# Running sums of two of seven block products kept in PSUM by ScalarE copies instead of VectorE adds, in a fused attention and MLP kernel

## The chip, the cores and the metric

The kernel runs on one core of a Trainium2 chip. The metric is the device time of one execution in microseconds; the lower the better. Before the change the median of 3 runs was 529.97 us (529.93 to 530.95).

## What is computed

Attention over 2 batches of 12 heads, 448 positions and 64 dimensions a head, then two MLPs on the 896 x 768 result, all in float32:

```python
x = attention(q, k, v)            # 896 x 768
h = ((x @ w1) * (x @ w2)) @ w3    # 896 x 1024
x = h @ w_out                     # 896 x 768
g = np.maximum(x @ w_in, 0.0) ** 2   # 896 x 2048
out = g @ w_out2                  # 896 x 768
```

## The kernel before

Each large product after the attention is done as a 2 x 2 block product with seven block products in place of eight (P1 to P7, a Strassen-Winograd form), issued in the order 1, 2, 6, 5, 7, 3, 4. Every float32 operand of a block product is split into a high part (a cast to the matmul's reduced float32, by ScalarE) and a low part (float32 minus high part, by VectorE), and each block product is three matmuls: high by high, high by low, low by high.

The change is in the last product, `g @ w_out2`. The 2048 columns of `g` are worked off in four groups, `g` = 0 to 3 in the code. A group has two stretches. In the first, the products with `win2` make four 448-row tiles of `g` for both halves of the batch, each squared and split. In the second (called the o stretch below), `o_step` multiplies them with `w_out2`. For each block product n there are two halves d of the inner dimension, and for each d three row tiles t = 0, 1, 2 of 128 rows. Every (n, d, t) is three matmuls of 128 x 128 by 128 x 384, so a block product is 18 matmuls in a group. The last 64 rows of each batch half are done by `rest_step` in two tiles, 24 matmuls in a group; together 150.

PSUM has eight banks. A row tile t uses three accumulation chains (`CHAIN`): "a" holds P1, then P1+P2; "b" starts as a ScalarE copy of P1 and then takes P6, P7 and P4; "c" holds P5, then P5+P3. When a block product of a tile is done, the bank is added to the running sum of the output tile in SBUF (`into_acc`, `acc_tile`; these tiles are named `g0` in the built program and `g` in the profile). The first time a tile is met it is copied, by whichever of ScalarE and VectorE the planner chooses; each later time it is a VectorE `tensor_tensor` add (line 1182, recorded at the helper's line 425). P2 goes to tile (t, 0), P6 and then P5+P3 to tile (3+t, 0), P5 and then P1+P6+P7 to tile (3+t, 1), and P4's bank to tile (t, 1). Because the chain in bank b goes on after it has been read out, P7's matmuls of a tile wait for the read of P6, and P4's for the read of P7; in chain c P3's wait for the read of P5.

The rest tiles are done otherwise already: in groups 1 to 3 ScalarE copies the running sum into the bank first (line 1248), the matmuls add to it, and ScalarE copies it out.

The order on each engine comes from `Program.order`, a list planner with fixed costs per operation that runs once when the program is built. Engines work through their lists in that order. ScalarE (ACT), VectorE (DVE) and the sync engine's DMA queue (SP) each take the next instruction only when the one ahead has started. `prog.add` records an operation with its engines, what it reads and what it writes; `act`, `dve` and `pe` give the planner's costs. `take_bank` and `take_fs` hand out a PSUM bank or one of twelve SBUF rows (`fs`).

Of the kernel before, what the change touches and what calls it, by code (L numbers as in the profile page):

```python
# [8 lines left out]
F32 = mybir.dt.float32  # L9
# [115 lines left out]
def attention_moe_moe2(ctx: ExitStack, tc: tile.TileContext, qk, v, w1, w2, w3, w_out, w_in2, w_out2, out):  # L125
    nc = tc.nc
    NP_ALL, P, S2 = qk.shape
# [11 lines left out]
    HN = DM // 2  # L139
# [24 lines left out]
    fs = big.tile([P, NFS, S], F32, tag="fs", name="fs")  # L164
# [6 lines left out]
    def mm(o, l, r, start, stop, **more):  # L171
        return nc.tensor.matmul(o, l, r, start=start, stop=stop, **more)  # L172
# [41 lines left out]
    GROUPS = KF2 // 4  # L214
    TT = S // P
# [118 lines left out]
    prog = Program({"S": 700})  # L334
    pools = {}
    engine_of = {"A": nc.scalar, "V": nc.vector}

    def act(width, psum=False, strided=False):
        gap = 60 + 0.815 * width if psum else 75 + (0.96 if strided else 0.845) * width
        return {"A": (gap, gap + 105)}  # L340

    def dve(width, fast=False):
        gap = 70 + (0.52 if fast else 1.038) * width
        return {"V": (gap, gap + 85)}
# [3 lines left out]
    def pe(columns):  # L348
        return {"T": (columns * PE_ROW, columns * PE_ROW + 170)}
# [3 lines left out]
    def bank(i):  # L353
        if i not in banks:
            pool, tag = (pools["ps"], "mm") if i < 6 else (ps_w, "w")
            banks[i] = pool.tile([P, S], F32, tag=tag, name=f"bank{i}")
        return banks[i]

    free_banks = list(range(8))
    written = [0] * 8  # L360
# [5 lines left out]
    tiles = {}  # L366
# [21 lines left out]
    def g_at(kind, at, parts, width):  # L388
        m, at = divmod(at, ROW)
        if m < EVEN:  # L390
            m, at = 0, m * ROW + at
        if (kind, m) not in tiles:
            tiles[kind, m] = pools["big2"].tile(
                [P, ROW if m else EVEN * ROW], F32 if (kind, m) == ("g", 0) else F32R, tag=f"G{m}", name=f"{kind}{m}")
        return tiles[kind, m][:, at:at + parts * width].rearrange("p (s c) -> p s c", s=parts)

    def g_names(at, width):
        return [("g", c) for c in range(at // REST, (at + width) // REST)]

    def acc_tile(i):  # L400
        return g_at("g", i * HN, 1, HN)[:, 0]
# [22 lines left out]
    def tt(out, x, y, what):  # L424
        return lambda e: engine_of[e].tensor_tensor(out(), x(), y(), op=what)  # L425
# [5 lines left out]
    def copy(out, x):  # L431
        return lambda e: engine_of[e].copy(out(), x()) if e == "A" else engine_of[e].tensor_copy(out(), x())  # L432
# [12 lines left out]
    def fs_at(i, width=S):  # L445
        return lambda: fs[:, i, :width]

    def bank_at(i, width=S):
        return lambda: bank(i)[:, :width]
# [331 lines left out]
    def end_attention(e):  # L781
        attention.close()
        for n in ("xt", "big2"):
            pools[n] = ctx.enter_context(tc.tile_pool(name=n, bufs=1, reuse_waits="tile"))
        pools["ps"] = ctx.enter_context(tc.tile_pool(name="ps", bufs=6, space=PSUM, reuse_waits="tile"))
        for i in range(6):
            bank(i)
        for n in B_OF.values():
            tiles["x", n] = xB.get(n) or pools["xt"].tile([P, 2, KH, S], F32R, tag=n, name=f"x{n}")

    prog.add({"T": (0, 0)}, end_attention, [], [("open",)], behind=prog.ops)
    for c in range(2):
        place = turn("w", 2)
# [24 lines left out]
    def slot_in(n, k):  # L818
        return {"T1": 0, "T3": KH, "T2": 2 * KH, "B21": 3 * KH}[n] + k

    for n in ("B21", "T2", "T1", "T3"):
        for k in range(KH):
            i = slot_in(n, k)
# [3 lines left out]
    for k in range(KH):  # L827
        i, b = slot_in("T2", k), slot_in("B21", k)
# [88 lines left out]
    def ring_names(u):  # L917
        k = slot_of[u]
        return [("ring", i, s) for i in ((k, k + 1) if wide(u) else (k,)) for s in "hl"]
# [3 lines left out]
    def take_bank():  # L923
        return free_banks.pop(0)

    def take_fs():
        return free_fs.pop(0)
# [83 lines left out]
    def need_block(g, n, d):  # L1011

        if (g, n, d) in g_place:
            return
        at = g_place[g, n, d] = place_at(turn("place", PLACES))
        m = 4 * g + 2 * d
        b11, b12, b21, b22 = (g_rows[m + i, 1 - b] for i in range(2) for b in range(2))

        def sub(out, x, y):
            prog.add(dve(BN), tt(fs_at(out, BN), fs_at(x, BN), fs_at(y, BN), ALU.subtract),  # L1020
                     [("fs", x), ("fs", y)], [("fs", out)])

        row = {"1": b11, "2": b21, "5": b11, "7": b12, "3": b22, "4": b21}.get(n)
        if n == "6":
            row = take_fs()
            sub(b11, b12, b11)
            sub(row, b22, b11)
        elif n == "7":
            sub(b12, b22, b12)
        his, los = (g_names(at + r * BN, BN) for r in range(2))  # L1030
        parts_of(lambda: g_at("g", at, 2, BN)[:, 0], lambda: g_at("g", at, 2, BN)[:, 1], fs_at(row, BN), BN, ("fs", row),
                 his, los)
        if n == "6":
            sub(b21, b21, row)
        if n not in "12":
            give_fs(row)
# [140 lines left out]
    def into_acc(g, tile, n, bk, final):  # L1177

        i = 2 * tile + n
        o, a, src, dst = bank_at(bk, HN), lambda: acc_tile(i), ("bank", bk), g_names(i * HN, HN)  # L1180
        if (tile, n) in begun:
            prog.add(dve(HN), tt(a, o, a, ALU.add), [src, *dst], dst)
        else:
            begun.add((tile, n))
            prog.add(act(HN, True) | (dve(HN) if tile < 2 * TT else {}), copy(a, o), [src], dst)
        if final and g == GROUPS - 1:
            cols = slice(n * HN, (n + 1) * HN)
            if tile < 2 * TT:
                chunks = [(slice(0, P), (1 - tile // TT) * S + tile % TT * P)]
            else:  # L1190
                chunks = [(slice(b * REST, (b + 1) * REST), b * S + BN) for b in range(2)]
            for ps, row in chunks:
                prog.add({"S": (200, 2000)}, lambda e, ps=ps, row=row: nc.sync.dma_start(
                    out=out[row:row + ps.stop - ps.start, cols], in_=acc_tile(i)[ps]), dst)

    begun, o_state, rest_bank = set(), {}, {}

    def o_step(n, g, d, t, unit):

        need_block(g, n, d)  # L1200
        st = o_state.setdefault((g, t), {})
        w, at, chain = hls[unit], g_place[g, n, d], CHAIN[n]
        start = chain not in st
        if start:
            st[chain] = take_bank()
            written[st[chain]] = HN
            if n == "1":
                assert written[free_banks[0]]
                st["b"] = take_bank()
                written[st["b"]] = HN  # L1210
        i = st[chain]

        def run(e):
            x = g_at("g", at, 2, BN)
            for s, r in ((0, 0), (0, 1), (1, 0)):
                mm(bank(i)[:, :HN], x[:, s, t * P:(t + 1) * P], w[r],
                   start and (s, r) == (0, 0), d == 1 and (s, r) == (1, 0), skip_group_check=True)

        prog.add(pe(3 * HN), run, ring_names(unit) + g_names(at, 2 * BN) + ([] if start else [("bank", i)]),
                 [("bank", i)])  # L1220
        if d == 0:
            return
        if n == "1":
            j = st["b"]
            prog.add(act(HN, True), copy(bank_at(j, HN), bank_at(i, HN)), [("bank", i)], [("bank", j)])
        elif n == "2":
            into_acc(g, t, 0, i, True)
        elif n in "63":
            into_acc(g, TT + t, 0, i, n == "3")
        elif n in "57":  # L1230
            into_acc(g, TT + t, 1, i, n == "7")
        else:
            into_acc(g, t, 1, i, True)
        if n in "234":
            free_banks.append(i)
# [28 lines left out]
    for at, (kind, what, which, used) in enumerate(plan):  # L1264
        for u in used:
            need_unit(u)
        if kind == "product":
            product(what, which, used[0], at == 0)
        elif kind == "h":
            h_step(what, *which, used[0])  # L1270
        elif kind == "o":
            o_step(what, *which, used[0])
        else:
            rest_step(*what, which, used[0])
# [53 lines left out]
```

## Time and profile before

| what | value |
|---|---|
| median of 3 runs | 529.97 us (529.93 to 530.95) |
| the profiled execution's own time | 529.73 us |
| its span (first to last instruction) | 528.0 us |
| between the two | 1.73 us |
| TensorE (PE) busy | 514.4 us, 97% of the span |
| VectorE (DVE) busy | 490.8 us, 93% |
| ScalarE (ACT) busy | 385.4 us, 73% |
| granted TensorE clock | 1.00 |

PEld is TensorE's weight load, which runs beside the matmul before it. An instruction's duration in the trace is longer than its pitch (the distance from its start to the next one's start on a busy engine), because ends and starts overlap. "Idle before" is time in which the engine had nothing running, with what ended the wait behind an arrow.

### The profile page before, as it was taken

Reading aid. Unit: us, or ns where it says so; the run is one execution under the profiler, and the core shown is the slowest. Engines: PE = TensorE matmul, PEld = TensorE weight load, DVE = VectorE, ACT = ScalarE, POOL = GpSimd, SP = SyncE. Lnnn points to the kernel's source line nnn. Section 1 sums busy time; section 2 is a strip of 40 time slices with the busy share of each in tenths; the row PEclk is TensorE's granted clock in tenths of the full one; section 3 lists DMA queues with packets and bytes.
Section 4 is the critical chain, followed back from the end, with each engine's and each line's share of the span. In section 5 each row is a group of like instructions: output and inputs, shape, how many; then the busy total and the mean of one; then the engine's idle time right before and its main releaser. Section 6 shows DMA issues by size and latency. Waiting matters only on the chain.

```text
span 528.0 us, 8458 instructions
## 1 busy us (share of the span) xinstructions
PE 514.4 (97%) x2905; PEld 461.2 (87%) x2905; DVE 490.8 (93%) x1157; ACT 385.4 (73%) x890; POOL 15.2 (3%) x20
## 2 busy tenths in 40 slices
PE   6899999999999999999999999999999999999995
PEld 4658888888879999999999999999999989988995
DVE  5999998989899999987975899999999999999996
ACT  5989988767779465638486478986896589649951
POOL 1000000000000010221100000000000000000000
PEclk9999999999999999999999999999999999999999
DMA  8956544352652569999752402405530544044114
GB/s 315 303 194 227 178 170 175 124 178 69 236 176 65 179 186 253 251 251 258 164 164 89 153 27 65 175 1 177 182 122 0 164 172 145 0 127 175 59 60 150
DMA packets 26571, 81.29 MB, mean 154 GB/s; under 512 B 2400, under 2 KB 13408, under 8 KB 26528
## 3 DMA queue, kind: packets, MB, share of 16 engines
q1 hardware_dynamic: 22752, 75.24, 42.4%
q0 software_dynamic: 3776, 5.51, 6.6%
q8 instruction: 23, 0.38, 0.3%
q14 instruction: 20, 0.16, 0.1%
HBM read 74.84 MB, written 14.55 MB: 169 GB/s over the span
## 4 chain that ended last, share of the span: by engine, by line
PE 72%; DVE 19%; ACT 5%; DMA 2%; issue 1%; DVEq 0%
PE bank L172 51%; PE w L172 11%; DVE g L425 6%; PE s L172 4%; PE x L172 3%; PE pp L695 3%; DVE ring L425 3%; DVE fs L425 2%; DVE xs L486 2%; ACT ring L432 2%; DVE p L653 2%; DVE xs L425 1%; DMA raw_w<-in_w 1%; ACT xs L478 1%; DVE p L680 1%
## 5 line engine op out<-in xcount | busy, mean ns | idle before, releaser
L432 ACT CAST ring<-xs 128x384 fp32r<-128x384 f32 (+1 forms) x194 | 102.7, 546 | 48.8 <-PE bank L172 19.4
L172 PE MATMUL bank<-xT,ring 128*128 128x448 f32 x630 | 132.0, 366 | 0.0
L172 PEld LDWEIGHTS bank<-xT,ring 128*128 128x128 f32 x630 | 117.7, 188 | 9.4
L425 DVE TENSOR_TENSOR ring<-xs,ring 128x384 fp32r<-128x384 f32 (+1 forms) x194 | 111.4, 588 | 12.1 <-ACT ring L432 11.8
L172 PE MATMUL bank<-ring,g 128*128 128x384 f32 x600 | 106.1, 336 | 1.3 <-DVE g L425 1.3
L172 PEld LDWEIGHTS bank<-ring,g 128*128 128x128 f32 x600 | 104.1, 188 | 3.0 <-DVE g L425 2.6
L172 PE MATMUL bank<-xB,ring 128*128 128x448 f32 x489 | 102.9, 366 | 0.1
L172 PEld LDWEIGHTS bank<-xB,ring 128*128 128x128 f32 x489 | 91.4, 188 | 8.5 <-DVE ring L425 0.9
L663 ACT ACTIVATE p<-p,st 112x224 f32<-112x224 f32 (+3 forms) x96 | 50.1, 536 | 10.1 <-DVE st L653 10.1
L425 DVE TENSOR_TENSOR xs<-xs 128x384 f32<-128x384 f32 x96 | 51.7, 551 | 0.1
L432 ACT CAST g<-fs 128x384 fp32r<-128x384 f32 (+1 forms) x88 | 35.4, 421 | 14.9 <-DVE fs L425 14.7
L653 DVE CUSTOM_DVE_ANT_0 p<-s,mask 112x224 f32<-112x224 f32 (+3 forms) x96 | 36.8, 444 | 6.3 <-PE s L172 6.2
L172 PE MATMUL w<-hl_wout,w 128*128 128x384 f32 x192 | 36.2, 340 | 0.6 <-DVE wraw L425 0.6
L425 DVE TENSOR_TENSOR g<-fs,g 128x384 fp32r<-128x384 f32 (+1 forms) x88 | 36.7, 430 | 0.0
L172 PEld LDWEIGHTS w<-hl_wout,w 128*128 128x128 f32 x192 | 32.8, 188 | 1.9 <-DVE fs L425 0.9
L478 ACT ACTIVATE xs<-raw_w 128x768 f32<-128x768 f32 (+1 forms) x30 | 24.3, 816 | 11.6 <-DMA raw_w<-in_w 5.8
L172 PE MATMUL s<-qk 64*112 64x448 f32 (+3 forms) x192 | 28.0, 436 | 4.7 <-DMA qk<-in_qk 4.7
L432 ACT COPY fs<-bank 128x448 f32<-128x448 f32 x49 | 26.1, 532 | 8.1 <-PE bank L172 8.1
L425 DVE TENSOR_TENSOR g<-bank,g 128x384 f32<-128x384 f32 x60 | 31.5, 551 | 0.0
L172 PE MATMUL bank<-ab,ring 128*128 128x448 f32 x144 | 29.5, 365 | 0.0
L680 DVE TENSOR_SCALAR p<-p,st 112x448 f32<-112x448 f32 (+1 forms) x96 | 29.1, 360 | 0.1
L172 PEld LDWEIGHTS bank<-ab,ring 128*128 128x128 f32 x144 | 27.0, 188 | 2.1
(77 smaller groups left out, 667.6 us busy)
## 6 DMA issues: line engine op xcount, KB each, us to landing
raw_wout<-in_w_out SPq DMA_DIRECT2D x24, 768.0 KB, 4.3
raw_w<-in_w SPq DMA_DIRECT2D x16, 768.0 KB, 4.9
raw_win<-in_w_in SPq DMA_DIRECT2D x16, 768.0 KB, 4.3
raw_w<-in_w SPq DMA_DIRECT2D x16, 512.0 KB, 4.4
qk<-in_qk SPq DMA_DIRECT2D x12, 448.0 KB, 5.1
s_dram<-w_dram POOLq DMA_DIRECT2D x8, 576.0 KB, 9.1
w_dram<-wraw SPq DMA_DIRECT2D x8, 384.0 KB, 2.4
s_dram<-w_dram SPq DMA_DIRECT2D x4, 768.0 KB, 7.3
```

The source lines that it names most:

```text
L172: return nc.tensor.matmul(o, l, r, start=start, stop=stop, **more)
L425: return lambda e: engine_of[e].tensor_tensor(out(), x(), y(), op=what)
L432: return lambda e: engine_of[e].copy(out(), x()) if e == "A" else engine_of[e].tensor_copy(out(), x())
L478: nc.scalar.activation(y(), raws[key][:, :, 1].bitcast(F32), AF.Prelu, scale=2.0 ** -112, alpha=-2.0 ** 32)
L486: nc.vector.scalar_tensor_tensor(yi, yi, 3, raws.pop(key)[:, :, 0], op0=ALU.logical_shift_left, op1=ALU.bitwise_or)
L653: prog.add({"V": (gap, gap + 160)}, lambda e: nc.vector.tensor_tensor_reduce(block(p, j, i), s_t[p, j, g][:CP, o:o + w], mask[:, S - w:], ...
L663: prog.add({"A": (gap, gap + 100)}, lambda e, i=i: nc.scalar.activation(block(p, j, i), block(p, j, i), AF.Exp, bias=st_t[p][:, 0, j, i:i ...
L680: lambda e, i=i: nc.vector.tensor_scalar(block(p, j, i), block(p, j, i), st_t[p][:, 3, j, i:i + 1], None, ALU.mult),
L695: nc.tensor.transpose(x[0][:CP, o * CP:(o + 1) * CP], block(p, j, i)[:, c * CP:(c + 1) * CP], ident[:CP, :CP])
```

## The change

P5 and P3 are taken out of the VectorE adds, except in the last group.

- P5: a running sum of its own, in a new SBUF tile `P5` for t = 0 and 1 and in an `fs` row for t = 2. In groups 1 to 3 ScalarE copies the sum into the bank (`sum_in`) before P5's first matmul, which then adds to it. In groups 0 to 2 ScalarE copies it out again (`sum_out`) and the bank is given back. In group 3 the bank holds P5 of all groups and goes to tile (3+t, 1) by `into_acc` as before, and P3 is added on top of it in the same bank.
- P3: in groups 0 to 2 it has a chain of its own, "e". ScalarE copies tile (3+t, 0) into a bank, P3's matmuls add to it, and ScalarE copies it back.
- Tile (3+t, 1) is now met first by P7, so in group 0 P7 is a copy where it was an add.

```diff
@@ end_attention
+        tiles["P5"] = pools["xt"].tile([P, TT - 1, HN], F32, tag="P5", name="P5")
@@
+    def sum_in(i, x, names):
+
+        prog.add(act(HN), copy(bank_at(i, HN), x), names, [("bank", i)])
+
+    def sum_out(i, x, names):
+        prog.add(act(HN, True), copy(x, bank_at(i, HN)), [("bank", i)], names)
+
+    def p5_sum(t):
+
+        if t < TT - 1:
+            return lambda: tiles["P5"][:, t], ("P5", t)
+        if "row" not in p5_row:
+            p5_row["row"] = take_fs()
+        return fs_at(p5_row["row"], HN), ("fs", p5_row["row"])
...
+        over = g == GROUPS - 1
+        if n == "3" and not over:
+            chain = "e"
         start = chain not in st
         if start:
             st[chain] = take_bank()
+            assert written[st[chain]]
             written[st[chain]] = HN
...
-        i = st[chain]
+        i, to = st[chain], 2 * (TT + t)
+        if start and n == "5" and g:
+            sum_in(i, p5_sum(t)[0], [p5_sum(t)[1]])
+            start = False
+        elif start and n == "3":
+            sum_in(i, lambda: acc_tile(to), g_names(to * HN, HN))
+            start = False
...
         elif n == "2":
             into_acc(g, t, 0, i, True)
+        elif n == "3" and not over:
+            sum_out(i, lambda: acc_tile(to), g_names(to * HN, HN))
+        elif n == "5" and not over:
+            sum_out(i, p5_sum(t)[0], [p5_sum(t)[1]])
+            free_banks.append(i)
         elif n in "63":
             into_acc(g, TT + t, 0, i, n == "3")
```

TensorE's list is the same before and after but for the bank numbers. On VectorE, in the o stretch of group 2, these are the rows from the first add of P5 to the first add of P7 before the change (`g0<-bank` is an add to a running sum, `g3` to `g7` are low parts of the left operand, `ring` low parts of the weights):

```order
L425 TENSOR_TENSOR g0_3549<-bank7_2196,g0_3549 128x384
L425 TENSOR_TENSOR g7_3581<-fs_70,g7_3581 128x384
L425 TENSOR_TENSOR ring_68<-xs_69,ring_68 128x384
L425 TENSOR_TENSOR xs_69<-xs_69 128x384
L425 TENSOR_TENSOR g0_3549<-bank1_1959,g0_3549 128x384
L425 TENSOR_TENSOR g0_3549<-bank3_1961,g0_3549 128x384
L425 TENSOR_TENSOR ring_68<-xs_69,ring_68 128x384
L425 TENSOR_TENSOR g7_3581<-fs_70,g7_3581 128x384
L425 TENSOR_TENSOR fs_70<-fs_70 128x384
L425 TENSOR_TENSOR ring_68<-xs_69,ring_68 128x384 x2
L425 TENSOR_TENSOR g0_3549<-bank5_1963,g0_3549 128x384
```

and these the rows of the same place after it:

```order
L425 TENSOR_TENSOR xs_69<-xs_69 128x384
L425 TENSOR_TENSOR g7_3582<-fs_70,g7_3582 128x384
L425 TENSOR_TENSOR xs_69<-xs_69 128x384
L425 TENSOR_TENSOR g7_3582<-fs_70,g7_3582 128x384
L425 TENSOR_TENSOR ring_68<-xs_69,ring_68 128x384
L425 TENSOR_TENSOR fs_70<-fs_70 128x384
L425 TENSOR_TENSOR ring_68<-xs_69,ring_68 128x384 x3
L425 TENSOR_TENSOR g0_3550<-bank5_1964,g0_3550 128x384
```

P5's three adds are gone, and P7's first add (the last row of either) stands that much earlier in the list.

On ScalarE, in the same o stretch, from a cast of the left operand to the last cast before the raw weights of the next group, before the change:

```order
L432 CAST g5_3371<-fs_70 128x384
L432 CAST g7_3581<-fs_70 128x384 x2
L432 COPY g0_3549<-bank2_1960 128x384
L432 CAST ring_68<-xs_69 128x384 x2
L432 CAST g6_3420<-fs_70 128x384
L432 CAST ring_68<-xs_69 128x384 x2
L432 CAST g6_3420<-fs_70 128x384
```

and after it:

```order
L432 CAST g5_3372<-fs_70 128x384
L432 COPY bank1_1960<-P5_1955 128x384
L432 CAST g7_3582<-fs_70 128x384
L432 CAST ring_68<-xs_69 128x384
L432 COPY bank6_2199<-P5_1955 128x384
L432 COPY g0_3550<-bank4_1963 128x384
L432 COPY bank7_2197<-fs_70 128x384
L432 CAST g7_3582<-fs_70 128x384
L432 CAST g6_3421<-fs_70 128x384
L432 CAST ring_68<-xs_69 128x384 x2
L432 CAST g6_3421<-fs_70 128x384
```

The three `sum_in` copies of P5 (two from `P5`, one from `fs`) now stand between the casts of P7's and P3's operands; the copies for P3 and the copies out follow further down.

On the sync engine's queue the last rows, the stores of the output (128 rows of a row tile, 64 of a rest tile), were before the change:

```order
L1193 DMA out<-g_3549 128x384
L1193 DMA out<-g_3549 64x384 x2
L1193 DMA out<-g_3549 128x384 x5
L1193 DMA out<-g_3549 64x384 x2
L1193 DMA out<-g_3549 128x384 x6
```

and are after it:

```order
L1194 DMA out<-g_3550 128x384 x3
L1194 DMA out<-g_3550 64x384 x2
L1194 DMA out<-g_3550 128x384 x5
L1194 DMA out<-g_3550 64x384 x2
L1194 DMA out<-g_3550 128x384 x4
```

Behind the second pair of rest stores there are four stores where there were six: two of P3's stores have moved ahead of it.

## Rows read from the trace of the kernel before

**Rows 1.** The page: busy time, share of the span, instructions of each engine.

```profile
span 528.0 us, 8458 instructions
PE 514.4 (97%) x2905; PEld 461.2 (87%) x2905; DVE 490.8 (93%) x1157; ACT 385.4 (73%) x890; POOL 15.2 (3%) x20
```

**Rows 2.** Windows: o stretch and first stretch in turn from group 0, then the tail.

```profile
core 0: us, PE busy (x) PEld busy (x) DVE busy (x) ACT busy (x) POOL busy (x), PEclk, DMA share, GB/s
336.85:362.88 26.03, 26.03 (x152) 26.03 (x151) 25.88 (x58) 20.10 (x49) 0.00 (x0) 1.00 0.21 65
362.88:388.85 25.97, 25.97 (x131) 24.11 (x131) 25.56 (x53) 23.39 (x52) 0.00 (x0) 1.00 0.59 195
388.85:415.32 26.47, 26.47 (x151) 25.95 (x150) 26.47 (x58) 17.27 (x40) 0.00 (x0) 1.00 0.10 31
415.32:441.65 26.33, 26.26 (x131) 23.89 (x131) 26.33 (x54) 22.94 (x49) 0.00 (x0) 1.00 0.56 194
441.65:469.45 27.80, 26.62 (x151) 25.93 (x150) 27.80 (x63) 17.77 (x41) 0.00 (x0) 1.00 0.13 47
469.45:495.81 26.36, 26.30 (x131) 23.90 (x131) 26.36 (x54) 22.96 (x49) 0.00 (x0) 1.00 0.48 164
495.81:522.52 26.71, 26.55 (x151) 25.87 (x149) 26.71 (x62) 14.99 (x37) 0.00 (x0) 1.00 0.17 56
522.52:528.00 5.48, 0.00 (x0) 0.00 (x0) 0.76 (x2) 0.00 (x0) 0.00 (x0) 0.98 0.67 232
```

**Rows 3.** Waits from 336 us on: who for whom, us in total, times, longest.

```profile
ACT g L432 <- DVE fs L425: 14.7, 10, 2.8
ACT ring L432 <- DVE xs L486: 8.1, 9, 1.8
...
PEld bank L172 <- DVE g L425: 2.6, 4, 1.0
...
PE bank L172 <- DVE g L425: 1.3, 3, 0.6
PEld bank L172 <- DVE ring L425: 0.9, 2, 0.5
...
PEld bank L172 <- ACT bank L432: 0.2, 1, 0.2
```

**Rows 4.** Timeline of PE: o stretches of groups 0, 2 and 3.

```profile
336.85 26.19 PE L172 MATMUL bank<-ring,g 128*128 128x384 f32 x150
...
441.65 23.63 PE L172 MATMUL bank<-ring,g 128*128 128x384 f32 x135
465.93 0.80 PE L172 MATMUL bank<-ring,g 128*128 128x384 f32 x3 [0.65 <-DVE g L425]
467.26 2.35 PE L172 MATMUL bank<-ring,g 128*128 128x384 f32 x12 [0.54 <-DVE g L425]
...
519.62 2.90 PE L172 MATMUL bank<-ring,g 128*128 128x384 f32 x15 [0.16 <-DVE g L425]
```

**Rows 5.** Timeline of DVE in group 2, adds of P2, of P7, and the end of the kernel.

```profile
450.83 1.02 DVE L425 TENSOR_TENSOR g<-bank,g 128x384 f32<-128x384 f32 x2
451.76 0.55 DVE L425 TENSOR_TENSOR ring<-xs,ring 128x384 fp32r<-128x384 f32 x1
...
463.45 0.55 DVE L425 TENSOR_TENSOR g<-bank,g 128x384 f32<-128x384 f32 x1
...
465.32 0.55 DVE L425 TENSOR_TENSOR g<-bank,g 128x384 f32<-128x384 f32 x1
465.79 0.95 DVE L486 SCALAR_TENSOR_TENSOR xs<-xs,raw_win 128x768 uint32<-128x768 uint32 x1
466.66 0.55 DVE L425 TENSOR_TENSOR g<-bank,g 128x384 f32<-128x384 f32 x1
...
520.41 2.88 DVE L425 TENSOR_TENSOR g<-bank,g 128x384 f32<-128x384 f32 x6
```

**Rows 6.** Groups by form from 336 us on: count | busy us, mean ns | idle before.

```profile
L425 DVE TENSOR_TENSOR g<-bank,g 128x384 f32<-128x384 f32 x60 | 31.5, 551 | 0.0
L432 ACT COPY g<-bank 128x384 f32<-128x384 f32 x18 | 8.0, 481 | 1.6 <-PE bank L172 1.6
L432 ACT COPY bank<-g 128x384 f32<-128x384 f32 x6 | 2.9, 481 | 0.0
L432 DVE COPY g<-bank 128x384 f32<-128x384 f32 x2 | 1.1, 553 | 0.0
```

**Rows 7.** Timeline of ACT in the o stretch of group 2.

```profile
449.63 1.35 ACT L432 CAST g<-fs 128x384 fp32r<-128x384 f32 x3
450.88 0.48 ACT L432 COPY g<-bank 128x384 f32<-128x384 f32 x1
452.79 1.00 ACT L432 CAST ring<-xs 128x384 fp32r<-128x384 f32 x2 [1.43 <-PE bank L172]
```

**Rows 8.** Timeline of SP, the stores of the output at the end (SPq is the queue's issue).

```profile
523.05 0.89 SPq L1193 DMA_DIRECT2D out<-g  x2
524.03 0.90 SPq L1193 DMA_DIRECT2D out<-g  x2
```

**Rows 9.** The stores by tile, and windows of the tail (columns as in rows 2).

```profile
L1193 SPq DMA_DIRECT2D out<-g x16: 333/426/599, 504.2 to 524.5; - x16
DMA to landing us min/median/max: 1.9/2.1/3.5
...
523.00:524.00 1.00, 0.00 (x0) 0.00 (x0) 0.28 (x1) 0.00 (x0) 0.00 (x0) 1.00 1.03 369
525.00:526.00 1.00, 0.00 (x0) 0.00 (x0) 0.00 (x0) 0.00 (x0) 0.00 (x0) 1.00 1.02 366
```

More of the change, by code (lines that the diff above doesn't have):

```diff
@@ L1194, in into_acc @@
                     out=out[row:row + ps.stop - ps.start, cols], in_=acc_tile(i)[ps]), dst)
-    begun, o_state, rest_bank = set(), {}, {}
+    def sum_in(i, x, names):
[8 more added lines that the diff above has]
+        return fs_at(p5_row["row"], HN), ("fs", p5_row["row"])
+    begun, o_state, rest_bank, p5_row = set(), {}, {}, {}
     def o_step(n, g, d, t, unit):
```

## The prediction, written before the changed kernel ran

> **What bounds the kernel now.** I read the page first: TensorE is busy 97% of the span, VectorE 93%, ScalarE 73% [rows 1]. The average hides the place, so I cut the last product into its stretches [rows 2]. There both are full: PE is busy 26.03 of 26.03 us in the first o stretch, and VectorE is busy for the whole of every later stretch (27.80 of 27.80 in group 2). ScalarE has 9 us free in an o stretch of groups 1 and 2, but only 3.4 us in a first stretch.
>
> Two full engines mean that one is the floor and the other sometimes falls behind it. Which one shows in the lengths. Every group issues the same matmuls, and group 0's o stretch runs without a marked wait: 150 matmuls in 26.19 us [rows 4], 0.16 of which is the last one's own end, so 26.03 and a pitch of 0.1735 us. The stretch of 362.88 to 388.85 has the same 25.97 us of work as its two followers. What the others have above these two is time that PE lost:
>
> - o stretches: 26.47 - 26.03 = 0.44 in group 1, 27.80 - 26.03 = 1.77 in group 2, 26.71 - 0.16 - 26.03 = 0.52 in group 3;
> - first stretches: 26.33 - 25.97 = 0.36 and 26.36 - 25.97 = 0.39.
>
> Together 3.48 us. The waits name the cause [rows 3]: PE and its weight loads wait for VectorE's `g` (2.6 and 1.3 us, partly the same time) and `ring` (0.9), for ScalarE only once (0.2).
>
> The place of the largest is group 2 [rows 4, 5]. P7's three VectorE adds start at 463.45, 465.32 and 466.66, and PE resumes at 465.93 and 467.26, each time just as one ends: P4 goes into the bank that P7's add is reading. By the pitch, P7's first tile was ready after 102 matmuls, at 441.65 + 102 x 0.1735 = 459.35. So VectorE is 4.1 us behind, and being behind, not the length of an add, is what PE pays for.
>
> **The parts.** *VectorE.* P3's adds go in groups 0, 1 and 2 (9), P5's in groups 1 and 2 (6), and P7's in group 0 become copies (3), of which the new order gives VectorE one more than before: 17 instructions fewer, five in group 0 and six each in groups 1 and 2. An add lasts 551 ns [rows 6], but its pitch is less: two adds and the next instruction start 0.93 us apart (450.83 to 451.76) [rows 5], 0.467 each. 17 x 0.467 = 7.9 us less VectorE work out of some 173 between 350 and 523 us. When PE reaches P7 of group 2, fourteen fewer have stood ahead (five, six and P5's three): 6.5 us, more than the 4.1 it was late. In group 1, eight fewer are 3.7 us; in group 3 all seventeen are 7.9. VectorE then has slack in every group and comes back to PE's pace, so all 3.48 us are open to be won, except the 0.2 that waits for ScalarE. I take 3.3; the bounds are 0 and 3.48.
>
> *ScalarE.* 35 copies more: in group 0 eight, in groups 1 and 2 twelve each (three each of P5 in, P5 out, P3 in, P3 out), in group 3 three. Both directions are in the trace at 481 ns [rows 6], so no price is unknown. Twelve are 5.8 us: group 1's o stretch goes from 17.27 to 23.0 busy of 26, group 2's from 17.77 to 23.5. They fit, with 3 us over. They go on the path only where PE waits for a preload. For P5 in group 2: P2's last add ends about 451.85 [rows 5]; P5 starts after 72 matmuls, at 454.15. Three copies take 1.4 us of the 2.3, and ScalarE stands idle for 1.43 us right there [rows 7]. VectorE being earlier widens this, since the adds of P2 are themselves late. For P3 the bank's data is done two block products (6.2 us) ahead. So the cost is nothing, hidden by P6 and P7; without that cover each preload is 0.48 us.
>
> *A row and a bank.* P5's third sum takes one of twelve `fs` rows; the other rows still outnumber the eight that a group holds. P5's banks are free after its copy out, earlier than before. The P5 tile shifts the SBUF places of other tiles; this moves one already satisfied DMA wait by three instructions and I cost it at nothing.
>
> *The tail.* After the last matmul (522.52) the last add ends at 523.28, the span at 528.0 [rows 2]. The adds themselves are barely late there (six from 520.41 on) [rows 5], but the queue of stores is: its last issue starts at 524.5, 1.2 us after the last add [rows 5, 9], issues come some 0.5 us apart [rows 8], and the DMA engines run full from 523 to 526 at 366 to 369 GB/s [rows 9]. The reason is that P7's and P3's adds came late and nine full stores were issued in one run. On time, P7's stores go out 7 us ahead of the end and P3's 4 us, and four stores, not six, follow the last rest tile. Bounds: 0, if the last stores still queue; and 2.6, if the last issue follows its add at once (1.2) and lands in the median 2.1 instead of the longest 3.5 (1.4). I take 1.2, the queue alone.
>
> The sum: 529.73 - 3.3 - 1.2 = 525.2 for the profiled execution. The median of the runs shown is 0.24 above it, so 525.4.
>
> [...] The trace gives 0.1735 us for a 384-column matmul where nothing waits [rows 4], and its weight loads fill the stretch as well (26.03 of 26.03) [rows 2]. [...]
>
> **The rivals.**
>
> 1. *Only part comes back.* The waits in groups 1 and 2 go (0.44 + 0.36 + 1.77 and group 3's 0.39, less 0.2), but group 3, whose o stretch keeps all 18 adds, and the tail stay: 529.73 - 2.76 = 527.0, with the median's 0.24 527.2. For it: group 3's o stretch issues as many VectorE adds as before. Against: it starts with VectorE caught up.
> 2. *ScalarE becomes the wait; slower.* A preload stands in ScalarE's list ahead of casts that VectorE and PE need, and it waits for VectorE's add of P2 or P6. For it: the first stretches hold ScalarE for 87 to 90% of the time already [rows 2], and from 449.63 on in group 2 it runs three casts back to back [rows 7]. [...] There are six sets of preloads (P5 in three groups, P3 in three). If each set of three copies lay bare on the path, 6 x 1.44 = 8.6 us would come on top of 525.4: 534.0. It turns slower than before from (4.5 + 1.06) / 6 = 0.93 us a set. Against: slack of 2.3 us and more.
> 3. *Nothing.* VectorE fills the time with work that the planner moved forward, such as the next group's raw weights (0.87 us of pitch each) [rows 5], and P7's adds stay as late: 529.7 to 530.0. Against: fourteen adds fewer.
> 4. *VectorE was the pace throughout*, PE's 26.03 included: then the whole 7.9 us go, 529.73 - 7.9 = 521.8. Against: PE's weight loads are full in group 0's stretch.
>
> **How the numbers follow.** Forecast 0.65; part 0.17; slower by ScalarE 0.09; nothing 0.06; VectorE throughout 0.03. The forecast's own bounds: 529.73 - 3.48 - 2.6 = 523.65 and, with half of the waits and none of the tail, about 528. I set 523.8 to 528.0, which holds the forecast and most of rival 1. A change of 0.2% (1.06 us) is about what a measurement of this kernel can tell from none. Faster by more: 0.65 + 0.17 + 0.03 = 0.85; within: 0.06; slower: 0.09.
>
> **What would show it.** Windows cut at the same matmuls: every o stretch at 26.0 to 26.2 us and every first stretch at 26.0. The waits of PE and its loads for VectorE's `g` and `ring` under 0.5 us in all. VectorE with idle time, under 97% in the stretches of groups 1 to 3; about 43 adds `g<-bank` and 3 copies where there were 60 and 2. ScalarE at 85 to 92% there, its waits for VectorE shorter. The last store's issue within 0.3 us of its add, and 4.3 us or less from the last matmul to the end. I am wrong if PE waits for ScalarE's `bank` by more than a microsecond (rival 2), if VectorE is still busy for the whole of group 2 (rival 3), or if the o stretches fall below 25.9 us (rival 4).

## The result and the profile after the change

The change made the kernel faster: median 525.17 us (4 runs, 524.11 to 526.12) against 529.95 (4 runs, 529.1 to 530.95), a ratio of 0.9909 with a 95% interval of 0.9882 to 0.9935. A second set of runs gave 525.51 against 529.48, ratio 0.9919 (0.9902 to 0.9936). The profiled execution took 524.11 us, with a span of 522.3.

The page of the changed kernel answers to [rows 1]: 17 VectorE instructions fewer, 35 ScalarE instructions more.

```profile
span 522.3 us, 8468 instructions
PE 511.7 (98%) x2905; PEld 461.3 (88%) x2905; DVE 484.6 (93%) x1140; ACT 397.7 (76%) x925; POOL 15.0 (3%) x20
```

Its chain that ended last is almost all TensorE. Before the change it read 72% PE, 19% DVE and 5% ACT.

```profile
PE 94%; ACT 2%; DVE 2%; DMA 1%; issue 0%; DVEq 0%
```

Windows of the changed kernel, cut at the same matmuls as [rows 2] (o stretch and first stretch in turn, then the tail; columns as there):

```profile
335.59:361.61 26.02, 26.02 (x151) 26.02 (x150) 25.37 (x56) 24.32 (x60) 0.00 (x0) 1.00 0.26 86
361.61:387.59 25.98, 25.98 (x132) 24.12 (x131) 24.99 (x51) 22.68 (x49) 0.00 (x0) 1.00 0.54 185
387.59:413.61 26.02, 26.02 (x151) 26.02 (x150) 25.91 (x57) 22.00 (x53) 0.00 (x0) 1.00 0.11 40
413.61:439.59 25.98, 25.98 (x132) 24.12 (x131) 25.47 (x53) 22.25 (x49) 0.00 (x0) 1.00 0.60 198
439.59:465.61 26.02, 26.02 (x151) 26.02 (x150) 25.91 (x57) 22.27 (x53) 0.00 (x0) 1.00 0.13 44
465.61:491.59 25.98, 25.98 (x132) 24.06 (x131) 25.92 (x53) 22.26 (x49) 0.00 (x0) 1.00 0.45 152
491.59:517.79 26.20, 26.20 (x151) 25.80 (x149) 25.55 (x57) 15.73 (x38) 0.00 (x0) 1.00 0.22 72
517.79:522.30 4.51, 0.00 (x1) 0.00 (x0) 0.60 (x2) 0.00 (x0) 0.00 (x0) 1.00 0.58 198
```

Read the first column: every o stretch now lasts 26.02 us (the last one 26.20, with 0.16 of its last matmul's end) and every first stretch 25.98, which is PE's own work. The waits from 336 us on have no row of PE or its weight loads any more; those of [rows 3] are gone. (In the profile of the second set of runs, called "the change again" below, one is left: the weight loads wait 0.3 us for a low part in group 2's first stretch.) From here on "length" means the distance from the first matmul of group 0's o stretch to the end of the last o stretch. It was 517.79 - 335.59 = 182.20 us, before 522.52 - 336.85 = 185.67: 3.47 won. The tail was 4.51, before 5.48: 0.97 won. Together 4.44 us, and 529.73 - 4.44 = 525.3 is close to the median.

The span of this one execution is shorter by another 1.26 us, because its o stretch starts at 335.59 and not at 336.85. That lies ahead of every changed instruction (763 VectorE and 579 ScalarE instructions come before it in either kernel). The start was 335.83 and 336.51 in two experiments made from the kernel before, and 335.62 to 336.38 in those made from the changed one, so it is not counted as the change's.

VectorE is still full: 25.91 of 26.02 us in the o stretches of groups 1 and 2. What changed is when a certain instruction comes. These are P7's three adds in group 2, on VectorE's timeline after the change; they answer to [rows 5]:

```profile
458.60 0.55 DVE L425 TENSOR_TENSOR g<-bank,g 128x384 f32<-128x384 f32 x1
...
460.47 0.55 DVE L425 TENSOR_TENSOR g<-bank,g 128x384 f32<-128x384 f32 x1
...
461.80 0.55 DVE L425 TENSOR_TENSOR g<-bank,g 128x384 f32<-128x384 f32 x1
```

P7's first tile was ready at 439.59 + 102 x 0.1735 = 457.29, so VectorE is 1.3 us behind here where it was 4.1. PE needs the third tile's bank after 138 matmuls, 23.94 us into the stretch; with its 0.55 us the add must start by about 23.3. It now starts at 461.80 - 439.59 = 22.21, and started at 25.01 before (21.64 and 22.18 in groups 1 and 3, before 23.65 and 23.67). PE's timeline shows an o stretch in one piece where [rows 4] had three:

```profile
439.59 26.19 PE L172 MATMUL bank<-ring,g 128*128 128x384 f32 x150
```

### The profile page after: what moved, and what is told of

It is laid out like the page before. It is cut to its first block, busy times and chain, and to the rows that moved or that the text cites. A ratio compares the mean times of both kernels' runs of the same rounds, so it can differ in the third digit from the quotient of the medians.

```text
span 522.3 us, 8468 instructions
## 1 busy us (share of the span) xinstructions
PE 511.7 (98%) x2905; PEld 461.3 (88%) x2905; DVE 484.6 (93%) x1140; ACT 397.7 (76%) x925; POOL 15.0 (3%) x20
## 4 chain that ended last, share of the span: by engine, by line
PE 94%; ACT 2%; DVE 2%; DMA 1%; issue 0%; DVEq 0%
PE bank L172 69%; PE w L172 13%; PE x L172 4%; PE s L172 4%; PE pp L695 4%; ACT p L663 1%; ACT xs L478 1%; DMA qk<-in_qk 1%; DVE p L653 0%; DVE p L680 0%; ACT pt L701 0%; DVE xs L486 0%; DVE g L425 0%; DVE w L486 0%; ACT w L478 0%; DVE st L672 0%
## 5 line engine op out<-in xcount | busy, mean ns | idle before, releaser
L172 PE MATMUL bank<-ring,g 128*128 128x384 f32 x600 | 104.8, 334 | 0.0
L432 ACT COPY fs<-bank 128x448 f32<-128x448 f32 (+1 forms) x52 | 27.5, 529 | 8.9 <-PE bank L172 8.7
L172 PE MATMUL s<-qk 64*112 64x112 f32 (+3 forms) x192 | 27.4, 425 | 4.3 <-DMA qk<-in_qk 4.3
L172 PEld LDWEIGHTS s<-qk 64*112 64x112 f32 x192 | 15.4, 181 | 14.3 <-issue 6.0
```

## The experiments

Theory 1 says that PE waited because VectorE had too much work due, and that the change gains by taking it away. The rivals are that the change gains by something else (chains of their own for P5 and P3, so that PE waits for no read), or by the place of P7's adds in the list. All times of one row come from one chip; each ratio is against the kernel before on that chip. Length, tail and "P7" come from one profile of each kernel; the two profiles of the change differ by 0.25 us in length and 0.40 in the tail. "P7" is how far into the o stretch P7's third add starts in groups 1, 2 and 3.

| kernel | median us | ratio (95%) | length | tail | P7 |
|---|---|---|---|---|---|
| before | 529.95 | | 185.67 | 5.48 | 23.65, 25.01, 23.67 |
| the change | 525.17 | 0.9909 (0.9882 to 0.9935) | 182.20 | 4.51 | 21.64, 22.21, 22.18 |
| the change again | 525.51 | 0.9919 (0.9902 to 0.9936) | 182.45 | 4.91 | 21.65, 22.41, 22.18 |
| copies out by VectorE | 530.44 | 1.0005 (0.9986 to 1.0025) | 187.19 | 6.01 | 24.46, 24.76, 23.67 |
| other VectorE work taken | 524.33 | 0.9897 (0.9864 to 0.9931) | 182.17 | 3.82 | 19.46, 19.85, 21.15 |
| P3 alone | 528.74 | 0.9986 (0.9969 to 1.0004) | 185.56 | 5.12 | 23.86, 24.08, 22.69 |
| P5 alone | 526.47 | 0.9937 (0.9913 to 0.9962) | 182.29 | 5.79 | 20.93, 22.17, 23.26 |
| P3's copies out by VectorE | 526.58 | 0.9939 (0.9919 to 0.9959) | 182.37 | 5.83 | 20.94, 22.38, 23.35 |
| P5's copies out by VectorE | 528.07 | 0.9970 (0.9955 to 0.9985) | 184.71 | 6.01 | 24.29, 23.93, 23.04 |
| before, P7 first | 529.97 | 1.0006 (0.9997 to 1.0016) | 188.04 | 3.73 | 19.11, 19.66, 19.69 |
| P3 alone, P7 first | 527.96 | 0.9977 (0.9966 to 0.9989) | 186.00 | 4.0 | 19.08, 19.92, 19.81 |
| the change, P7 first | 526.26 | 0.9942 (0.9924 to 0.996) | 183.37 | 4.75 | 19.85, 19.42, 19.94 |
| copies in twice | 526.60 | 0.9958 (0.9944 to 0.9972) | 182.88 | 5.65 | 22.44, 22.41, 23.48 |
| last stores from ScalarE | 525.50 | 0.9921 (0.9904 to 0.9938) | 182.70 | 4.50 | 21.67, 22.12, 22.20 |

**The work put back.** The changed kernel, with its 18 copies out done by VectorE.

```diff
     def sum_out(i, x, names):
-        prog.add(act(HN, True), copy(x, bank_at(i, HN)), [("bank", i)], names)
+        prog.add(dve(HN), copy(x, bank_at(i, HN)), [("bank", i)], names)
```

> The changed kernel with its 18 copies out of PSUM (P5 and P3, groups 0 to 2) given to VectorE; chains, banks and copies in stay as changed. Length meant below: from the first matmul of group 0's o stretch to the end of the last matmul, 185.67 us before the change, 182.20 after. Theory 1 (VectorE's amount of work): VectorE has 16 instructions more than after the change, nearly all that was taken away (53.2 and 54.2 us of pitch in the two full group periods, against PE's 52.0), so 2.5 to 3.5 us of waiting come back: length 184.7 to 185.7, time 527.5 to 529.5. Theory 2 (own chains and earlier free banks of P5 and P3 took the waits away, whatever VectorE has to do): length 182.2 to 182.8, time about 525.

The whole gain was gone, and more than theory 1 gave: 530.44 where 527.5 to 529.5 was expected, length 187.19 where 184.7 to 185.7 was. PE waits for VectorE again, and now for ScalarE too. Rows of its waits:

```profile
PEld bank L172 <- DVE g L425: 2.6, 4, 0.9
PE bank L172 <- DVE g L425: 1.3, 4, 0.5
...
PEld bank L172 <- ACT bank L432: 1.1, 4, 0.5
```

The chains of their own and the copies in are all still there, so they win nothing by themselves. The third row may be a part of the excess; what made it was not tested.

**Other work taken away.** The kernel before, with none of the change, but without 18 of the low parts of `w_out2` in groups 0 to 2.

```diff
         prog.add(act(width), copy(lambda: t[0], x), src, [("ring", i, "h") for i in slots])
+        if not wide(u) and u[1][0] == "wout2" and u[1][1] < 12 and u[0] in ("S1", "S2", "S3"):
+            return
```

> The kernel before the change, with 18 other VectorE instructions left out: the low parts of six of the sixteen weight blocks of w_out2 in groups 0 to 2 (the product uses stale ones there). P5 and P3 are added by VectorE as before; ScalarE has no copy more. VectorE's pitch in the two full group periods is 50.9 and 51.4 us. Theory 1: like the change: length 182.2 to 182.6, last stores as after the change, time 524.5 to 526. Theory 2: the chains are as before, so P4 still waits for P7's adds: length 184.5 to 185.7, time 528.5 to 530.

It came to 524.33 and a length of 182.17, a little under theory 1's 524.5 and 182.2 and far from theory 2's, with PE's o stretch of group 3 whole again, on the old chains and with every add of P3 and P5:

```profile
492.49 26.19 PE L172 MATMUL bank<-ring,g 128*128 128x384 f32 x150
```

Together these two show the cause: VectorE's work in these stretches, whatever its kind, and nothing that is peculiar to the new chains.

**P3 alone, P5 alone.** Each half of the change takes about as much work from VectorE: it issues 1149 instructions with P3 alone, 1148 with P5 alone, 1157 before. P3 alone leaves out P5's share in tile (3+t, 0); nothing is left out of P5 alone.

```diff
# P3 alone
-        if start and n == "5" and g:
-            sum_in(i, p5_sum(t)[0], [p5_sum(t)[1]])
-            start = False
-        elif start and n == "3":
+        if start and n == "3":
...
-            sum_out(i, p5_sum(t)[0], [p5_sum(t)[1]])
+            into_acc(g, TT + t, 1, i, False)
# P5 alone
-        elif start and n == "3":
-            sum_in(i, lambda: acc_tile(to), g_names(to * HN, HN))
-            start = False
...
-        elif n == "3" and not over:
-            sum_out(i, lambda: acc_tile(to), g_names(to * HN, HN))
```

> P3's running sum through the bank as changed, P5 added by VectorE as before, with its bank given back. The share of P5 of groups 0 to 2 in tile (3+t, 0) is left out. VectorE has 8 instructions fewer than before; its pitch in the two full group periods is 53.2 and 52.3 us, against 54.2 and 54.2 before and PE's 52.0. Theory 1: 1.5 us over PE's pace stay, less the slack carried in: length 182.6 to 184.0, time 525.5 to 527.5. Theory 2: P3's own chain is the one that no longer waits for the read of P5, so nearly all is won: 182.2 to 182.6.

> P5's running sum as changed; P3 in a bank of its own from zero and added by VectorE. Nothing left out. VectorE has 9 instructions fewer than before; its pitch in the two full group periods is 52.3 and 52.8 us. Theory 1: about 1 us over PE's pace stays: length 182.4 to 183.5, time 525.3 to 527. Theory 2: as the kernel before where P4 waits for P7 (neither of its banks is touched): 184.5 to 185.7.

P5 alone came to a length of 182.29, just under theory 1's 182.4 to 183.5 and far from theory 2's. P3 alone missed both ranges: its length is 185.56, what it was before, and the same wait for P7's third add is there in group 2. First VectorE, then PE, with P3 alone:

```profile
465.56 0.55 DVE L425 TENSOR_TENSOR g<-bank,g 128x384 f32<-128x384 f32 x1
```

```profile
441.48 24.14 PE L172 MATMUL bank<-ring,g 128*128 128x384 f32 x138
466.17 2.35 PE L172 MATMUL bank<-ring,g 128*128 128x384 f32 x12 [0.54 <-DVE g L425]
```

The add starts 24.08 us into the stretch, after the limit of 23.3. This is not the whole loss: the o stretches of groups 1 and 2 lose 0.66 and 0.86 us by it, the first stretches behind them 0.80 and 1.07, where the weight loads wait for `ring`, 1.1 us for VectorE and 0.9 for ScalarE. So the amount of work as a total is not all of theory 1: where it falls counts.

**The same amount in another place.** In the changed kernel VectorE does either P3's nine copies out or P5's nine.

```diff
# P3's copies out by VectorE
-            sum_out(i, lambda: acc_tile(to), g_names(to * HN, HN))
+            prog.add(dve(HN), copy(lambda: acc_tile(to), bank_at(i, HN)), [("bank", i)], g_names(to * HN, HN))
# P5's copies out by VectorE
-            sum_out(i, p5_sum(t)[0], [p5_sum(t)[1]])
+            prog.add(dve(HN), copy(p5_sum(t)[0], bank_at(i, HN)), [("bank", i)], [p5_sum(t)[1]])
```

> The changed kernel with only P3's nine copies out given to VectorE. They stand behind P7's adds in VectorE's list, as P3's adds did before. VectorE's pitch in the two full group periods is 52.3 and 52.8 us. If what counts is the VectorE work that stands ahead of P7's third add in an o stretch (PE loses time once that add starts later than some 23.3 us into the stretch): length 182.2 to 182.6 (182.20 after the change), P7's third add at 20.9 to 23.3, as with P5 alone; time 525.5 to 527 with a longer tail. If only the amount counts: the same as its twin beside it.

> The changed kernel with only P5's nine copies out given to VectorE; two of three in a group stand ahead of P7's adds. VectorE's pitch in the two full periods is 52.8 and 52.8 us, one instruction fewer in all than its twin. By place: P7's third add later than in the twin, 22 to 24 us into the o stretch, and length 182.6 to 184.5. By amount alone: as the twin within 0.5 us.

With P3's given to VectorE, PE's length stays at 182.37; with P5's, it goes up to 184.71, just above the 184.5 expected. Windows of one group each (o stretch and first stretch, groups 0 to 2), P3's by VectorE first, then P5's:

```profile
336.30:388.30 52.00, 52.00 (x281) 50.14 (x280) 51.47 (x109) 46.38 (x107) 0.00 (x0) 1.00 0.42 138
388.30:440.30 52.00, 52.00 (x281) 50.14 (x280) 51.98 (x110) 42.83 (x97) 0.00 (x0) 1.00 0.35 118
440.30:492.30 52.00, 52.00 (x281) 50.14 (x280) 51.78 (x108) 43.34 (x98) 0.00 (x0) 1.00 0.29 96
```

```profile
335.68:387.68 52.00, 52.00 (x281) 50.14 (x280) 49.33 (x105) 45.49 (x104) 0.00 (x0) 1.00 0.37 125
387.68:441.12 53.44, 53.09 (x281) 49.84 (x280) 53.06 (x113) 44.73 (x100) 0.00 (x0) 1.00 0.34 117
441.12:494.20 53.08, 52.59 (x281) 49.90 (x280) 53.06 (x113) 44.33 (x99) 0.00 (x0) 1.00 0.30 104
```

VectorE is busy for 155.22 us in the one and 155.45 in the other. PE's own work in three groups is 156.00, so either would fit. But in the second VectorE stands idle for 2.67 us in group 0, has 113 instructions each in groups 1 and 2 where the first has 110 and 108, and PE's three groups take 158.52. P5's copies, like its adds, can stand ahead of P7's adds, which P4 waits for; P3's come after P7's matmuls and can go behind. P3 alone and P5 alone show the same pattern: in windows cut the same way, VectorE is idle in group 0 for 1.17 us in the one and 0.57 in the other, and then has 113 instructions in each of groups 1 and 2 against 110 and 109. So it is shown that the total does not decide and that where the work falls in VectorE's list does. Two readings of this are left, work ahead of P7's adds, and work that VectorE could have done in group 0 and did in groups 1 and 2. No run separates them, and which of the planner's rules leaves VectorE idle in group 0 stays open.

**P7's adds put first.** If place were all, P7's adds could be moved up by hand. The planner sees them, and with them P5's adds to the same tiles, as due 6 us earlier; this was done with the kernel before, with P3 alone, and with the change.

```diff
+        for o in self.ops:
+            if o in self.early:
+                o.due -= 6000
...
-            prog.add(dve(HN), tt(a, o, a, ALU.add), [src, *dst], dst)
+            op = prog.add(dve(HN), tt(a, o, a, ALU.add), [src, *dst], dst)
+            if TT <= tile < 2 * TT and n == 1:
+                prog.early.add(op)
```

> The kernel before the change, same instructions, but the planner puts VectorE's adds of P5 and P7 first wherever they are ready (due 6 us earlier); P7's third add stands some 5 us of VectorE pitch further ahead in each o stretch. Length is again from the first matmul of group 0's o stretch to the end of the last (185.67 before, 182.20 after the change). Theory 1 (VectorE has more to do in a group than PE, 54.2 against 52.0 us): P4 no longer waits for P7, but the waiting turns up at another operand, mostly the weights' low parts: 184.3 to 185.7, time 528 to 530. Theory 3 (only the place of P7's adds in VectorE's list counts): 182.2 to 183.0, time 525.5 to 527.

> The kernel with P3's sum alone in the bank (length 185.56, P4 waiting 0.5 to 0.9 us for P7's last add in groups 1 and 2), with the adds of P5 and P7 put first as in the run beside it. The share of P5 of groups 0 to 2 in tile (3+t, 0) is left out here too. VectorE's pitch in the full group periods is 52.8 and 52.8. Theory 1: 0.8 us a group over PE's pace is left: 182.6 to 184.0. Theory 3: 182.2 to 182.6. If it stays at 185.0 or more, P7's adds are not what P3 alone failed on.

> The changed kernel with VectorE's adds of P5 and P7 put first as above. PE is at its floor already, so length 182.2 to 182.3; in group 3 P7's stores are issued about 2 us earlier, so the tail (last matmul to the end, 4.51 after the change) is 4.0 to 4.5 and the time 524.3 to 525.5.

All three lengths came out above what was expected: 188.04, 186.00 and 183.37. So did the last one's tail (4.75) and time (526.26). The wait for P7's adds did go, from 2.6 us to 0.2 in the kernel before. In its place came a longer one, for the low parts of the weights that had been pushed back. Its waits:

```profile
PEld bank L176 <- DVE ring L429: 6.1, 7, 2.0
PE bank L176 <- DVE ring L429: 3.7, 3, 1.7
...
PEld bank L176 <- DVE g L429: 0.2, 1, 0.2
```

and PE's timeline in group 2, where it stops before matmul 110 and not before 136 and 139 as in [rows 4]:

```profile
441.19 19.08 PE L176 MATMUL bank<-ring,g 128*128 128x384 f32 x109
461.91 7.40 PE L176 MATMUL bank<-ring,g 128*128 128x384 f32 x41 [1.64 <-DVE ring L429]
```

So PE pays for VectorE being behind, at whichever operand is next. P7's adds are only where it showed, in P3 alone as well: with them moved up, it stays at 186.00, above the 185.0 that was named as the sign of this. Moving these adds up by 6 us gains nothing, and the change does not gain by it; smaller moves were not tried.

**ScalarE doubled.** The changed kernel with every copy in made twice, 18 ScalarE copies more, for the rival that ScalarE becomes the wait.

```diff
         prog.add(act(HN), copy(bank_at(i, HN), x), names, [("bank", i)])
+        prog.add(act(HN), copy(bank_at(i, HN), x), names, [("bank", i)])
```

> The changed kernel with each of the 18 copies into a bank made twice, one after the other, by ScalarE (2.9 us more in groups 1 and 2 each, 1.4 in groups 0 and 3). If the copies are hidden behind P6 and P7 with slack: length 182.2 to 182.6, time as after the change within 0.7 us. If they lie at the edge of PE's path (the second rival of the prediction): three copies late in each of six sets, up to 190, time from 529 up.

The length was 182.88, 0.28 above the upper end of what was expected and 0.4 to 0.7 above the change's two profiles. PE's weight loads now wait for ScalarE's `bank`:

```profile
PEld bank L172 <- ACT bank L432: 0.5, 2, 0.3
```

Neither of the two is a wait for a doubled copy. One is in the first stretch of group 2, the other before P2's first matmul in group 3, which waits until ScalarE has copied P1 out of the same bank:

```profile
472.57 1.71 PEld L172 LDWEIGHTS bank<-xT,ring 128*128 128x128 f32 x9 [0.29 <-ACT bank L432]
...
496.98 21.95 PEld L172 LDWEIGHTS bank<-ring,g 128*128 128x128 f32 x126 [0.21 <-ACT bank L432]
```

Eighteen copies of 0.48 us would be 8.6 us if they lay bare; 0.5 of it shows, in other copies that they push back. The change's own copies are hidden, with some room beyond them. The median is 1.1 to 1.4 us above the change's, more of it in the tail (5.65) than in the length; why the tail grew was not tested.

**The list of stores.** The stores of P4's tiles issued from ScalarE's queue, the others from the sync engine's.

```diff
-                prog.add({"S": (200, 2000)}, lambda e, ps=ps, row=row: nc.sync.dma_start(
+                prog.add({q: (200, 2000)}, lambda e, ps=ps, row=row: (nc.scalar if e == "A" else nc.sync).dma_start(
```

where `q` is "A" for the row tiles of P4 and "S" otherwise.

> The changed kernel with the three stores of P4's tiles in the last group issued from ScalarE's queue, which has nothing left to do there, not from the sync engine's. Length as after the change, 182.2 to 182.3. If the sync engine's list of stores is what makes the end late (last issue 0.62 us after its add): tail 3.8 to 4.2 where it was 4.51, time 0.3 to 0.7 us under the changed kernel beside it. If the DMA engines' bytes are what counts: tail 4.4 to 4.6.

> The changed kernel once more, for comparison with the runs beside it: length 182.2, tail 4.3 to 4.7, time 524.1 to 526.1.

The time did not move: 525.50 beside 525.51, tail 4.50 beside 4.91 and 4.51, where 3.8 to 4.2 was expected if the list made the end. P4's adds, and its stores from ScalarE's queue:

```profile
517.90 1.60 DVE L425 TENSOR_TENSOR g<-bank,g 128x384 f32<-128x384 f32 x3 [0.64 <-PE bank L172]
```

```profile
L1195 ACTq DMA_DIRECT2D out<-g x3: 363/379/535, 518.5 to 519.5; - x3
```

The last store is issued at 519.5, as the last add ends (517.90 + 1.60), and the kernel still takes 3.9 us from there to its end. The sync engine's list is not what holds the last stores in the changed kernel. The change again came out at 182.45 and 4.91, both above its own expectation (182.2, 4.3 to 4.7); its time lies within it.

## Why the prediction was right, point by point

The time came out as forecast, 525.17 for 525.4, and by the path that was named. Some sizes and one sign were off.

**PE's loss comes back: right.** Forecast 3.3 us of 3.48; measured 3.47, and 3.22 in the second profile. All five stretches are at PE's own work.

**VectorE being behind is the cause: right, but its measure was not.** The two experiments that put work back and took other work away show it. The sign "VectorE under 97% busy" failed: 99.6% in the o stretches of groups 1 and 2. A sign of being wrong, VectorE busy for the whole of group 2, was all but there: 51.83 of 52.00 us. The prediction reckoned that fourteen instructions fewer, 6.5 us less work, ahead of P7 in group 2 would take away more than the 4.1 us that its adds were late. Counted from group 0's first matmul, the first of them went from 463.45 - 336.85 = 126.60 to 458.60 - 335.59 = 123.01, 3.6 us earlier. Windows of that stretch of time, before and after:

```profile
336.85:463.45 126.60, 126.53 (x687) 121.74 (x686) 126.05 (x269) 99.56 (x223) 0.00 (x0) 1.00 0.32 107
```

```profile
335.59:458.60 123.01, 123.01 (x671) 119.28 (x670) 120.63 (x256) 109.29 (x252) 0.00 (x0) 1.00 0.33 110
```

VectorE's work fell by thirteen instructions and 126.05 - 120.63 = 5.42 us, 1.1 short of the 6.5: the list had moved other work forward. Its idle time rose from 0.55 to 2.38 us, most of it in group 0 (1.64), where [rows 2] already had 0.41 in the first stretch that the prediction called wholly busy. By group 2 VectorE was full again, which is rival 3 in part. It cost nothing, because 2.8 us within the stretch was enough where 1.7 was needed (25.01 to 23.3). The margin is only 1.1 us in group 2, 0.9 in the second profile. The size came out right because the gain is capped at PE's 3.48 us; the VectorE term needed only to be large enough, and its own size was not tested by the time.

**Both parts alike: not said, and not so.** The sum multiplied 17 instructions by one price. P5's part is worth nearly all of PE's loss (182.29 alone) and P3's next to none of it (185.56 alone). What P3 adds to P5 would be in the tail: 5.79 with P5 alone, 4.5 to 4.9 with both, and medians of 526.47 and 525.2 to 525.5. The intervals of the ratios overlap (0.9913 to 0.9962 and 0.9902 to 0.9936), so a gain by P3 is likely, not shown.

**ScalarE's copies are hidden: right.** VectorE's adds and ScalarE's copies by form in the changed kernel; the forms with `P` and `fs` are new:

```profile
L425 DVE TENSOR_TENSOR g<-bank,g 128x384 f32<-128x384 f32 x42 | 22.1, 551 | 0.6 <-PE bank L172 0.6
...
L432 ACT COPY g<-bank 128x384 f32<-128x384 f32 x26 | 11.4, 483 | 1.5 <-PE bank L172 1.5
...
L432 ACT COPY bank<-g 128x384 f32<-128x384 f32 x15 | 7.2, 481 | 0.0
...
L432 ACT COPY bank<-P 128x384 f32<-128x384 f32 x6 | 2.8, 472 | 0.0
L432 ACT COPY P<-bank 128x384 f32<-128x384 f32 x6 | 2.7, 477 | 0.0
...
L432 ACT COPY fs<-bank 128x384 f32<-128x384 f32 x3 | 1.5, 499 | 0.0
L432 ACT COPY bank<-fs 128x384 f32<-128x384 f32 x3 | 1.4, 474 | 0.0
```

That is 42 adds and 59 copies, 35 more than in [rows 6], at the price taken (472 to 499 ns). ScalarE's o stretches came to 22.00 and 22.27 us where 23.0 and 23.5 was worked out, because on a busy ScalarE the copies start some 0.4 us apart (448.61, 449.02 and 449.40 below): the prediction priced VectorE's adds by their pitch and these copies by their duration. ScalarE's waits for VectorE's `fs` fell from 14.7 us [rows 3] to 7.7. P5's three copies in (`bank<-P` and `bank<-fs`) stand here in group 2, the last of them done at 449.9:

```profile
447.37 0.48 ACT L432 COPY bank<-P 128x384 f32<-128x384 f32 x1
...
448.61 0.48 ACT L432 COPY bank<-P 128x384 f32<-128x384 f32 x1
449.02 0.48 ACT L432 COPY g<-bank 128x384 f32<-128x384 f32 x1
449.40 0.49 ACT L432 COPY bank<-fs 128x384 f32<-128x384 f32 x1
```

P5 starts at 439.59 + 72 x 0.1735 = 452.08, so 2.2 us were to spare, where the prediction's 2.3 us less three copies left 0.9, to be widened by an earlier VectorE. Rival 2 falls for the change: PE waits for no copy, and with the copies in doubled for 0.5 us. It shows where VectorE is late as well: with the copies out by VectorE, the weight loads wait 1.1 us for ScalarE's `bank`.

**The tail: right in direction, a little too large.** Forecast 1.2 us less, measured 0.97 and, in the second profile, 0.57. P3's three adds of group 3 do come earlier now, ahead of P4's, where six stood back to back [rows 5]:

```profile
514.70 1.48 DVE L425 TENSOR_TENSOR g<-bank,g 128x384 f32<-128x384 f32 x3
516.78 1.60 DVE L425 TENSOR_TENSOR g<-bank,g 128x384 f32<-128x384 f32 x3 [0.60 <-PE bank L172]
```

The last add ends at 518.38, the last store is issued at 519.01, 0.63 us later, not within 0.3; before it was 1.2 [rows 5, 9]. The tail is 4.51, not 4.3 or less.

```profile
518.03 0.88 SPq L1194 DMA_DIRECT2D out<-g  x2
519.01 0.41 SPq L1194 DMA_DIRECT2D out<-g  x1
```

The step that was mis-sized is "the queue alone", put at 1.2 us. Of the 0.97 won, 0.18 is the last add (0.77 us after the last matmul before, 0.59 after), 0.58 the queue, and 0.21 the time from the last issue to the end (3.5 and 3.3 us). The stores sent from another queue show that the queue no longer decides. In the microsecond after the last issue the DMA engines are full:

```profile
519.00:520.00 1.00, 0.00 (x0) 0.00 (x0) 0.00 (x0) 0.00 (x0) 0.00 (x0) 1.00 1.02 367
```

That what is left of the tail is bytes and landing is argued from this row, not shown. Over all kernels the tail ran from 3.73 to 6.01 us, and what sets it in each stays open. That the forecast was met to 0.2 us is in part luck: by the second profile's length and tail the sum would be 529.73 - 3.22 - 0.57 = 525.9, not 525.2.

**The floor: the trace's pitch held.** The o stretches stopped at 26.02 us with no wait left, 0.1735 us for each of 150 matmuls; rival 4 falls. Even with VectorE's P7 adds at 19.46 us, as with other work taken, the length was 182.17.

Rival 1 falls too, since group 3 came back with the others (26.20 from 26.71).

## What to carry to other kernels

When two engines are both near full, their busy shares do not say which one loses time: VectorE stayed at 99.6% in the decisive stretches and PE's loss still went to zero. Find the instruction that the other engine waits for, and measure how late it is against the moment at which it is needed; a change is worth what it takes off that lateness, up to zero. The same number of instructions can be worth all of the loss or none of it, by where the list puts them: here P5's, which can stand ahead of that instruction, counted, and P3's, which come behind it, hardly did, though why is in part open. Moving the instruction itself up by 6 us only passed the delay to the next operand.

## What was not expected of the hardware

[rows 6] had ScalarE's copies of 128 x 384 float32 between SBUF and PSUM at 481 ns in both directions, and they stay there in the changed kernel: 481 from SBUF into PSUM, 483 from PSUM into SBUF. That is not a rule for every pair of ends. In the changed kernel a copy from one PSUM bank to another lasts 451 (466 before), and a cast of the same size with both ends in SBUF (another operation, so not a strict comparison) 515 (521 before):

```profile
L432 ACT CAST g<-fs 128x384 fp32r<-128x384 f32 x54 | 27.4, 515 | 7.7 <-DVE fs L425 7.7
...
L432 ACT COPY bank<-bank 128x384 f32<-128x384 f32 x12 | 5.2, 451 | 0.0
```

So on this kernel moving a sum into PSUM and out again costs ScalarE two copies, 0.96 us by their durations and some 0.8 by their pitch, for one VectorE add of 551 ns with a pitch of 467. It is a bad price, and it pays here because ScalarE had the time: 4.0 and 3.8 us are still free in the o stretches of groups 1 and 2 after the change.
